# First late pair: the rectifications on ScalarE, and the next pair's inputs asked for within the fifth product

## The chip, the cores and the metric

One core of a Trainium2 chip runs the whole kernel. The metric is the device time of one execution in microseconds. The kernel before takes 769.24 us, the median of three runs (768.65 to 773.24).

## What is computed

Linear attention with a decay per head, then a block that mixes with a Fourier transform, normalises each row and applies a two-layer perceptron. All inputs are float32: q, k and v of 4 x 8 x 768 x 64, and weights of 512 x 2048 and 2048 x 512. Cut to what matters here:

```
x = attention(q, k, v, lam)                  # (4, 768, 512)
u = x + real(fft2(x))                        # over positions and channels
un = (u - mean(u)) / sqrt(var(u) + 1e-6)
out = u + maximum(un @ w_ch1, 0) @ w_ch2
```

The change lies in the last line, in the rectification `maximum(..., 0)` and in the loads of the transposed un.

## The kernel before

**The work.** The 4 x 768 rows are 24 tiles of 128 rows, taken as 12 groups of two tiles. The first four groups ("plain") go through the perceptron by direct products, interleaved with attention and Fourier mixing. The other eight ("late") make four pairs of groups, handled at the end of the kernel by `late()`. They multiply by a scheme of seven products in place of eight (Strassen's, in Winograd's form): matrices are cut into quarters, sums of quarters are formed beforehand, and the seven products are added up in a few PSUM banks.

**The first late pair** (number 0) uses one level of that scheme in its first layer, `first_layer`, lines 1223 to 1289. It loops over HF = 8 column blocks i of the hidden layer. `prod` (L1230) issues a product of 256 columns: two matmuls in the program, four matmul instructions in the trace. For each block there are three PSUM banks, X, Y and Z, and seven products:

- `begin(i)`: a11 b11 into X, which ScalarE copies out (L1251); a12 b21 into Y, which VectorE adds to that copy (L1253) and rectifies in place (L1254). The result is the quarter a11 of the hidden layer.
- the body of the loop: s2 t2 on top of X, copied out by ScalarE (L1268); s3 t3 into Z; s1 t1 on top of X, copied out by ScalarE (L1271); VectorE adds Z to that copy (L1272) and rectifies it (L1273): the quarter a22.
- `finish(i)`, one block later: s4 b22 on top of X, read with a rectification by ScalarE into a tile sv (L1240): the quarter a21; a22 t4 on top of Z, which VectorE adds to the copy of L1268 (L1242) and rectifies (L1243): the quarter a12. Then come two sums on VectorE that the second layer needs, a21 + a22 (L1244) and a11 - a21 (L1245).

Since X and Z are written on top of what they hold, TensorE may go on in such a bank only when its last reader, on ScalarE or VectorE, is through. Three blocks are begun ahead. Beside this, `keep_sums` has POOL form the sums of the second layer's weights (L1054, L1058), one set of four instructions in each of seven blocks, and SP sends them to DRAM.

**The second layer** of a pair is seven products, `deep_second(j, k)` with k from 0 to 6, each of seven small matmul groups (`seven`, L1397; a group is eight matmul instructions in the trace). After each group the function `read` takes the result out of PSUM: by a ScalarE copy (L1403) where it is the first of its target, otherwise by a VectorE add (L1405). `in_step` starts a new product every seven steps and lets the last three groups of one alternate with the first groups of the next.

**The second pair's inputs.** From product 2 of the first pair on, `read` also advances `sums_of_first`: sums of first-layer weights, eight VectorE instructions (L320) in the tile `ur`, of which six are written to DRAM by POOL's queue (L322). A sum is issued after the first, third and fifth of every seven reads. `load_u(j + 1)` then asks for the second pair's inputs, 1 MB in two requests on SP's queue (L1093), into a new tile of the same name and the same place as `ur`; it must therefore wait until those writes are done. In the kernel before it stands at the end of product 4 (k == 4), after `run(P.sums)` has used up what was left of the sums. The first VectorE instruction on these inputs is L1140, in `inputs`. SP's queue also carries the loads of three tiles `tx` for every product (`load_three`, L1104) and three writes of sums into w (`place_sums_w`, L1070).

**What sets the order.** Semaphores and the order of each engine's queue come from the Tile framework, whose planner picks by its own estimate of when each instruction becomes ready, with the written order as the priority. In the trace the order is therefore not always the written one: L1242 is written ahead of L1244 and L1245 and runs behind them. Only what is passed to `keep` (`tc.keep_in_program_order`) is pinned. Among the pinned are L1140, the loads of `place_sums_w`, and POOL's work in `keep_sums`.

Of the kernel before, what the change touches and what calls it, by code (L numbers as in the profile page):

```python
# [16 lines left out]
AF = mybir.ActivationFunctionType  # L17
ALU = mybir.AluOpType
# [59 lines left out]
def kernel(  # L78
# [10 lines left out]
    nc = tc.nc  # L89
# [51 lines left out]
    def keep(i):  # L141

        if id(i) not in pinned:
            pinned[id(i)] = i
            tc.keep_in_program_order(i)
        return i
# [4 lines left out]
    def new(pool, shape, tag, **kw):  # L151
        cnt[0] += 1
        return pool.tile(shape, F32, tag=tag, name=f"{tag}{cnt[0]}", **kw)
# [854 lines left out]
    V = nc.vector  # L1008
# [75 lines left out]
    def load_u(j, queue=nc.sync):  # L1084

        r = s2.u[j] = new(s2.up, [128, 2, KO, G * 128], "ur")
        two = LATE[2 * j:2 * j + 2]
        for h, (b, g) in enumerate(two):
            if j == PAIRS - 1:
                for i in range(G):  # L1090
                    queue.dma_start(r[:, h, :, 128 * i:128 * i + 128], utd[two[i]][:, :, 128 * h:128 * h + 128])
                continue
            i = queue.dma_start(r[:, h], utd[b, g])  # L1093
            if j == 0:
                keep(i)

    def bank():
        return new(s2.ps, [128, DM], "p2")
# [81 lines left out]
    def load_x(j):  # L1180
        P = pairs[j]
        P.us = [new(s2.yp, [128, G, DM], "u2", bufs=2) for _ in range(2)]
        for k in range(2):
            for s in range(G):
                keep(nc.sync.dma_start(P.us[k][:, s], ud[P.who[k][s]]))
# [6 lines left out]
    def split(t):  # L1192

        A11, _, A21, _ = quarters_a(t)
        keep(V.tensor_tensor(A21, A11, A21, op=SUB))
# [27 lines left out]
    def first_layer(j):  # L1223

        P = pairs[j]
        h, U = P.h, P.U

        def prod(ps, a, b, i, first):
            for kt in range(2):
                nc.tensor.matmul(ps, lhsT=s2.A[a][:, kt, 128 * i:128 * i + 128], rhs=U[b][:, kt, :],  # L1230
                                 start=(first and kt == 0), stop=(kt == 1), skip_group_check=True)

        def two(t):
            return t.rearrange("p (s k) -> p s k", s=G)

        def finish(i, X, Z):
            a11, a12, a22, s1, s3 = (h[n][:, :, i, :] for n in ("a11", "a12", "a22", "s1", "s3"))
            prod(X, "s4", "b22", i, False)
            a21 = new(s2.hp, [128, G, 128], "sv", bufs=3)
            nc.scalar.activation(a21, two(X), AF.Relu)  # L1240
            prod(Z, "a22", "t4", i, False)
            V.tensor_tensor(a12, two(Z), a12, op=ADD)  # L1242
            V.tensor_scalar(a12, a12, 0.0, None, op0=ALU.max)  # L1243
            V.tensor_tensor(s1, a21, a22, op=ADD)  # L1244
            V.tensor_tensor(s3, a11, a21, op=SUB)  # L1245

        def begin(i):
            a11 = h["a11"][:, :, i, :]
            X, Y = (bank()[:, 0:G * 128] for _ in range(2))
            prod(X, "a11", "b11", i, True)  # L1250
            nc.scalar.copy(a11, two(X))  # L1251
            prod(Y, "a12", "b21", i, True)
            V.tensor_tensor(a11, two(Y), a11, op=ADD)  # L1253
            V.tensor_scalar(a11, a11, 0.0, None, op0=ALU.max)  # L1254
            return X

        last = None
        AHEAD = 3
        begun = [begin(i) for i in range(AHEAD)]
        for i in range(HF):  # L1260
            a12, a22 = (h[n][:, :, i, :] for n in ("a12", "a22"))
            if i >= AHEAD:
                begun.append(begin(i))
            X, Z = begun[i], bank()[:, 0:G * 128]
            if last:
                finish(*last)
            prod(X, "s2", "t2", i, False)
            nc.scalar.copy(a12, two(X))  # L1268
            prod(Z, "s3", "t3", i, True)
            prod(X, "s1", "t1", i, False)  # L1270
            nc.scalar.copy(a22, two(X))  # L1271
            V.tensor_tensor(a22, two(Z), a22, op=ADD)  # L1272
            V.tensor_scalar(a22, a22, 0.0, None, op0=ALU.max)  # L1273
            last = (i, X, Z)
            if i < len(PRODUCTS):
                if i == 0:
                    keep(nc.gpsimd.tensor_copy(s2.begun, h["a11"][:, 0, 0, 0:1]))
                keep_sums(i)
            if i == HF - 3:
                load_x(j)  # L1280
            if i == HF - 2:
                for k in range(2):
                    run(prepare_b(j, k))
            if i > HF // 2:
                split(h[("a11", "a12", "s3")[i - HF // 2 - 1]])
        run(prepare_a(j, 0))
        finish(*last)
        run(prepare_a(j, 1))
        open_y(j)
# [91 lines left out]
    def deep_second(j, k):  # L1381

        P = pairs[j]
        h, (a, b) = P.h, PRODUCTS[k]
        y11, y12, y21, y22 = P.y
        if k == 0:
            P.t = new(s2.yp, [128, G, HM], "t2")
        T = P.t
        y, fresh = ((T, 1), (y11, 1), (y22, 1), (T, 0), (y12, 1), (y21, 0), (y12, 0))[k]
        A11, A12, A3, A22 = [[t[:, i] for i in range(HF // 2)] for t in quarters_a(h[a])]  # L1390
        B11, T3, B21, B22 = quarters_b(s2.B[b])
        (S1, S2, S4), (T1, T2, T4) = P.pre_a.pop(k), P.pre_b.pop(k)
        ab = [(A11, B11), (A12, B21), (S2, T2), (A3, T3), (S1, T1), (A22, T4), (S4, B22)]

        def mm(m, ps, start):
            for i in range(HF // 2):
                nc.tensor.matmul(ps[:, 0:HM // 2], lhsT=ab[m][0][i], rhs=ab[m][1][:, i, :], start=(start and i == 0),  # L1397
                                 stop=(i == HF // 2 - 1), skip_group_check=True)

        def read(ps, s, m, first):  # L1400
            o = y[:, s, m * HM // 2:(m + 1) * HM // 2]
            if first and fresh:
                nc.scalar.copy(o, ps[:, 0:HM // 2])  # L1403
            else:
                V.tensor_tensor(o, ps[:, 0:HM // 2], o, op=ADD)  # L1405
            P.reads = P.reads + 1
            if P.sums and P.reads % 7 in (1, 3, 5):
                next(P.sums, None)

        if k == 0:  # L1410
            P.reads, P.sums = 0, None
        if j < DEEP and k == 2:
            P.sums = sums_of_first()
        yield from seven(mm, read, (0, 2, 3, 5, 4, 1, 6) if (j, k) == (PAIRS - 1, 6) else range(7))

        def add_u(o, y, k, m):
            u = P.us[k][:, :, 0:HM] if m == 0 else P.us[k][:, :, DM - 1:HM - 1:-1]
            nc.gpsimd.tensor_tensor(o, y, u, op=ADD)  # L1418

        who, yt = P.who, P.yt  # L1420
        if k == 0:
            h["s2"] = h["a11"]
            if j < DEEP:
                split(h["s1"])
            part_sum(V, h["a11"], h["s1"], h["a11"], SUB)
        elif k == 1:
            V.tensor_tensor(y11, y11, T, op=ADD)  # L1427
            add_u(y11, y11, 0, 0)
        elif k == 2:
            if j < DEEP:  # L1430
                split(h["a22"])
            h["s4"] = h["a12"]
            part_sum(V, h["a12"], h["a12"], h["s2"], SUB)
            if j == DEEP - 1:
                place_sums_w()
        elif k == 3:
            V.tensor_tensor(y22, y22, T, op=ADD)
            add_u(y21, y22, 1, 0)
            add_u(T, T, 0, 1)
            add_u(y22, y22, 1, 1)  # L1440
        elif k == 4:
            V.tensor_tensor(y22, y22, y12, op=ADD)
            V.tensor_tensor(y12, y12, T, op=ADD)
            if j < DEEP:
                run(P.sums)
                load_u(j + 1)
        elif k == 5:
            store(*who[1][1], yt[:, 1, 1])
            if j == PAIRS - 1:
                store(*who[1][0], yt[:, 1, 0])  # L1450
                for s in range(G):
                    store(*who[0][s], yt[:, 0, s], slice(0, HM))
        else:
            store(*who[0][1], yt[:, 0, 1], slice(HM if j == PAIRS - 1 else 0, DM))
            if j == PAIRS - 1:
                for m in (0, HM // 2):
                    store(*who[0][0], yt[:, 0, 0], slice(HM + m, HM + m + HM // 2))
            else:
                store(*who[1][0], yt[:, 1, 0])
                store(*who[0][0], yt[:, 0, 0])  # L1460
# [88 lines left out]
    def run(gen):  # L1549
        return sum(gen)  # L1550
# [116 lines left out]
```

## Time and profile before

| | |
|---|---|
| median of three runs | 769.24 us (768.65 to 773.24) |
| the profiled execution's own time | 765.44 us |
| its span on the core | 763.7 us |
| mean granted TensorE clock | 0.999 |
| TensorE busy | 740.6 us, 97% |
| VectorE busy | 606.2 us, 79% |
| ScalarE busy | 209.2 us, 27% |
| POOL busy | 202.5 us, 27% |
| HBM | 160 GB/s over the span |

The span is one execution as the hardware profiler saw it, and the time of 765.44 us holds it and 1.7 us around it. PE is TensorE's matmul, PEld its weight load, DVE is VectorE, ACT ScalarE, SP the queue that issues most transfers. Tiles are named without numbers: ha and hs are quarters of the hidden layer, p is a PSUM bank, y and t are the second layer's results, tx, td and sd are sums of weights in SBUF and in DRAM, ur is the pair's input, utd its source in DRAM. The first layer of the first late pair runs from 401.2 to about 451 us of the span, its second layer to about 495 us. In a timeline row the columns are start, length, engine, line, operation, written and read tiles with their shapes and count, and in brackets the idle time before it with what ended it.

### The profile page before, as it was taken

To read this page: it belongs to the slowest core of one execution; us is meant where nothing else is said; L and a number is where in the kernel's file an instruction comes from. 1 tells how busy PE (TensorE), PEld (TensorE's weight loads), DVE (VectorE), ACT (ScalarE), POOL (GpSimd) and SP (SyncE) were. 2 spreads that over 40 slices of the span, in tenths; PEclk is the share of its full clock that TensorE was granted. 3 is DMA by queue.
4 is the path that set the end of the run, shared out by engine and by line. 5 is a ranking of instruction groups with operands and counts; after the bars stand their busy time and mean duration, and the time that the engine had idled before them with its cause. 6 is when DMAs were issued, how large, how long until landed. Compare 5 with 4: busy or idle time off the path is not lost.

```text
span 763.7 us, 17114 instructions
## 1 busy us (share of the span) xinstructions
PE 740.6 (97%) x6890; PEld 643.9 (84%) x6890; DVE 606.2 (79%) x1162; ACT 209.2 (27%) x487; POOL 202.5 (27%) x221
## 2 busy tenths in 40 slices
PE   7889999999999999999999999999999999999997
PEld 6788888884576586769648899999999999999997
DVE  5668967659999787587937999779986699748984
ACT  3354554553142111012002221034301341034310
POOL 3444433210042223300007922350024001320013
PEclk9999999999999999999999999999999999999999
DMA  9879986536353537522522476675645456456452
GB/s 202 247 179 228 241 247 187 176 103 190 97 168 130 127 115 207 142 93 56 124 56 97 152 221 215 220 247 180 189 125 181 142 163 190 131 170 187 140 139 69
DMA packets 132741, 123.50 MB, mean 162 GB/s; under 512 B 67007, under 2 KB 93247, under 8 KB 132663
## 3 DMA queue, kind: packets, MB, share of 16 engines
q1 hardware_dynamic: 126902, 103.66, 48.0%
q0 software_dynamic: 4032, 12.99, 5.0%
q10 hardware_dynamic: 1728, 5.77, 2.4%
q8 instruction: 54, 0.88, 0.5%
q14 instruction: 25, 0.20, 0.1%
HBM read 90.66 MB, written 31.73 MB: 160 GB/s over the span
## 4 chain that ended last, share of the span: by engine, by line
PE 47%; DVE 3%; DMA 2%; issue 1%; POOL 0%; SPq 0%; ACT 0%; DVEq 0%; POOLq 0%
PE p L1397 21%; PE p L1323 17%; PE p L1230 6%; PE pm L960 4%; DMA sd<-ur 1%; DMA ur<-utd 1%; DVE w1s L1036 1%; DMA tx<-td 0%; DVE un L792 0%; DVE e L807 0%; POOL rs L771 0%; DVE stt L766 0%; DVE hs L1245 0%; DVE hr L952 0%; DVE ha L1273 0%
## 5 line engine op out<-in xcount | busy, mean ns | idle before, releaser
L960 PE MATMUL pm<-w,hr 128*128 128x512 f32 x240 | 105.8, 594 | 0.1
L945 PE MATMUL pm<-ut,w 128*128 128x256 f32 x448 | 101.2, 380 | 1.1 <-ACT ut L871 0.7
L945 PEld LDWEIGHTS pm<-ut,w 128*128 128x128 f32 x448 | 84.0, 190 | 15.3 <-issue 3.3
L960 PEld LDWEIGHTS pm<-w,hr 128*128 128x128 f32 x240 | 44.9, 190 | 54.4 <-issue 50.9
L1418 POOL TENSOR_TENSOR y<-y,u 128x512 f32<-128x512 f32 x12 | 19.9, 1661 | 186.8 <-DVE y L1427 100.4
L1397 PE MATMUL p<-tx,sx 128*128 128x128 f32 x400 | 52.7, 275 | 0.0
L1397 PEld LDWEIGHTS p<-tx,sx 128*128 128x128 f32 x400 | 48.6, 192 | 0.0
L1332 DVE TENSOR_TENSOR ha<-p,ha 128x512 f32<-128x512 f32 x60 | 40.1, 685 | 8.3 <-PE p L1323 8.1
L1403 ACT COPY y<-p 128x128 f32<-128x128 f32 x48 | 12.8, 266 | 103.6 <-PE p L1397 103.1
L1405 DVE TENSOR_TENSOR y<-p,y 128x128 f32<-128x128 f32 x92 | 25.5, 284 | 16.1 <-PE p L1397 9.4
L954 ACT ACTIVATE hr<-pm 128x256 f32<-128x256 f32 x40 | 15.4, 385 | 81.9 <-PE pm L945 79.9
L1397 PE MATMUL p<-w,ha 128*128 128x128 f32 x288 | 37.4, 275 | 0.0
L1332 DVE TENSOR_TENSOR hs<-p,hs 128x512 f32<-128x512 f32 x39 | 26.2, 685 | 12.3 <-PE p L1323 12.3
L1397 PEld LDWEIGHTS p<-w,ha 128*128 128x128 f32 x288 | 34.9, 192 | 0.1
L267 ACT ACTIVATE e<-e,cvt 128x512 uint16<-128x512 uint16 x32 | 22.9, 721 | 40.4 <-DVE e L266 36.5
L1323 PE MATMUL p<-sx,tx 128*128 128x128 f32 x264 | 33.9, 275 | 0.0
L1323 PEld LDWEIGHTS p<-sx,tx 128*128 128x128 f32 x264 | 31.7, 192 | 0.0
L934 POOL DMA_INDIRECT out_dram<-y,ix x12 | 15.0, 1251 | 62.7 <-DVE y L997 50.7
L623 POOL DMA_INDIRECT fo<-xa,ix x6 | 15.4, 2566 | 59.1 <-DVE w L271 53.8
L1323 PE MATMUL p<-ur,w 128*128 128x128 f32 x216 | 28.0, 275 | 0.0
L435 PE MATMUL pa<-w 64*64 64x128 f32 x768 | 25.5, 271 | 2.3 <-issue 2.0
L1330 ACT COPY ha<-p 128x512 f32<-128x512 f32 x24 | 14.0, 584 | 49.2 <-PE p L1323 49.2
(342 smaller groups left out, 1932.2 us busy)
## 6 DMA issues: line engine op xcount, KB each, us to landing
tx<-td SPq DMA_DIRECT2D x84, 256.0 KB
tx<-sd SPq DMA_DIRECT2D x63, 256.0 KB
words<-in_moe_w_ch_dram SPq DMA_DIRECT2D x23, 512.0 KB
w<-in_v_dram SPq DMA_DIRECT2D x12, 512.0 KB
words<-in_k_dram SPq DMA_DIRECT2D x11, 512.0 KB
td<-tx SPq DMA_DIRECT2D x21, 256.0 KB
raw<-in_moe_w_ch_dram ACTq DMA_DIRECT2D x9, 512.0 KB
ud<-x SPq DMA_DIRECT2D x16, 256.0 KB
```

Of the source, the lines that this page charges most:

```text
L267: P(nc.scalar.activation(pw, pw, AF.Relu, bias=cvt[:, 0:1], scale=8.0))
L435: lead(P(mm(pss[r][hi][HD[ch], hp, :], lhsT=kT[HD[hi], r, hp, D * ch:D * ch + D], rhs=qT[HD[hi], hp, C * ch:C * ch + C], start=True, stop= ...
L623: P(gather(out=eo[b][a][1][0:n, 1, 0:DM], out_offset=None, in_=xa[:, :], in_offset=row_of(a, n)))
L945: P(nc.tensor.matmul(ps, lhsT=w1[:, c, 128 * fc:128 * fc + 128], rhs=ut[:, c, :], start=(c == 0), stop=(c == KO - 1)))
L954: P(nc.scalar.activation(t, ps, AF.Relu))
L960: return P(nc.tensor.matmul(ps, lhsT=hr[(fc - f0) // 4][:, fc % 4, 128 * i:128 * i + 128], rhs=w2[:, fc, :], start=(fc == f0), stop=(fc == ...
L1230: nc.tensor.matmul(ps, lhsT=s2.A[a][:, kt, 128 * i:128 * i + 128], rhs=U[b][:, kt, :], start=(first and kt == 0), stop=(kt == 1), skip_gro ...
L1323: nc.tensor.matmul(ps[:, 128 * i:128 * i + 128], lhsT=ab[m][0][:, 128 * i:128 * i + 128], rhs=ab[m][1], start=(start and i == 0), stop=Tru ...
L1332: V.tensor_tensor(o, p, o, op=ADD)
L1397: nc.tensor.matmul(ps[:, 0:HM // 2], lhsT=ab[m][0][i], rhs=ab[m][1][:, i, :], start=(start and i == 0), stop=(i == HF // 2 - 1), skip_grou ...
L1405: V.tensor_tensor(o, ps[:, 0:HM // 2], o, op=ADD)
L1418: nc.gpsimd.tensor_tensor(o, y, u, op=ADD)
```

## The change

Two things. First, the three in-place rectifications of `first_layer`, each issued eight times, are issued as a ScalarE activation (Relu) in place of a VectorE `tensor_scalar` with max. Second, `load_u(j + 1)` leaves the end of product 4: `read` now calls it at the first of its turns at which `sums_of_first` has nothing left. By the written order that is the last read of product 3, which alternates with product 4's; the end of product 4 keeps only an assertion.

```
--- before
+++ after
@@ first_layer, finish @@
             prod(Z, "a22", "t4", i, False)
             V.tensor_tensor(a12, two(Z), a12, op=ADD)
-            V.tensor_scalar(a12, a12, 0.0, None, op0=ALU.max)
+            nc.scalar.activation(a12, a12, AF.Relu)
             V.tensor_tensor(s1, a21, a22, op=ADD)
             V.tensor_tensor(s3, a11, a21, op=SUB)
@@ first_layer, begin @@
             V.tensor_tensor(a11, two(Y), a11, op=ADD)
-            V.tensor_scalar(a11, a11, 0.0, None, op0=ALU.max)
+            nc.scalar.activation(a11, a11, AF.Relu)
             return X
@@ first_layer, the loop @@
             V.tensor_tensor(a22, two(Z), a22, op=ADD)
-            V.tensor_scalar(a22, a22, 0.0, None, op0=ALU.max)
+            nc.scalar.activation(a22, a22, AF.Relu)
             last = (i, X, Z)
@@ deep_second, read @@
             P.reads = P.reads + 1
-            if P.sums and P.reads % 7 in (1, 3, 5):
-                next(P.sums, None)
+            if P.sums and P.reads % 7 in (1, 3, 5) and next(P.sums, P) is P:
+                P.sums = None
+                load_u(j + 1)
@@ deep_second @@
             V.tensor_tensor(y12, y12, T, op=ADD)
             if j < DEEP:
-                run(P.sums)
-                load_u(j + 1)
+                assert P.sums is None
         elif k == 5:
```

More of the change, by code (lines that the diff above doesn't have):

```diff
@@ L1242, in finish @@
             V.tensor_tensor(a12, two(Z), a12, op=ADD)
-            V.tensor_scalar(a12, a12, 0.0, None, op0=ALU.max)
+            nc.scalar.activation(a12, a12, AF.Relu)
             V.tensor_tensor(s1, a21, a22, op=ADD)
@@ L1253, in begin @@
             V.tensor_tensor(a11, two(Y), a11, op=ADD)
-            V.tensor_scalar(a11, a11, 0.0, None, op0=ALU.max)
+            nc.scalar.activation(a11, a11, AF.Relu)
             return X
@@ L1272, in first_layer @@
             V.tensor_tensor(a22, two(Z), a22, op=ADD)
-            V.tensor_scalar(a22, a22, 0.0, None, op0=ALU.max)
+            nc.scalar.activation(a22, a22, AF.Relu)
             last = (i, X, Z)
@@ L1406, in read @@
             P.reads = P.reads + 1
-            if P.sums and P.reads % 7 in (1, 3, 5):
-                next(P.sums, None)
+            if P.sums and P.reads % 7 in (1, 3, 5) and next(P.sums, P) is P:
+                P.sums = None
+                load_u(j + 1)
         if k == 0:
@@ L1444, in deep_second @@
             if j < DEEP:
-                run(P.sums)
-                load_u(j + 1)
+                assert P.sums is None
         elif k == 5:
```

## The prediction

> **What bounds the kernel now.** I read the page first, then the two stretches that the diff touches in the windows view, then the timeline and the chain of waits inside them.
>
> ```profile
> PE 740.6 (97%) x6890; PEld 643.9 (84%) x6890; DVE 606.2 (79%) x1162; ACT 209.2 (27%) x487; POOL 202.5 (27%) x221
> ...
> 401.20:451.50 50.30, 49.68 (x233) 43.26 (x232) 45.91 (x73) 12.01 (x32) 39.09 (x30) 1.00 0.48 167
> 451.50:475.00 23.50, 23.50 (x213) 23.50 (x212) 22.70 (x44) 3.46 (x13) 3.74 (x5) 1.00 0.52 163
> 475.00:492.00 17.00, 15.65 (x140) 15.46 (x140) 11.23 (x25) 0.80 (x3) 5.25 (x5) 1.00 0.75 252
> ```
>
> TensorE is busy for 97% of the span. The columns of the windows rows are the stretch, then PE, PEld, DVE, ACT, POOL. The first row is the first pair's first layer: VectorE works 45.91 of its 50.30 us, ScalarE only 12.01, yet PE is idle for just 50.30 - 49.68 = 0.62. The third row holds the second layer's end and the arrival of the second pair: PE is idle for 17.00 - 15.65 = 1.35. Those two idle times are nearly all that these stages can give back. A saving on VectorE counts only where it ends one of them. The clock column is 1.00 in all three.
>
> The two stalls, in the order of time:
>
> ```profile
> 412.65 1.49 DVE L1245 TENSOR_TENSOR hs<-ha,sv 128x256 f32<-128x256 f32 x1
> 413.49 0.37 ACT L1271 COPY ha<-p 128x256 f32<-128x256 f32 x1 [2.21 <-PE p L1230]
> 413.94 0.84 PEld L1230 LDWEIGHTS p<-ur,w1s 128*128 128x128 f32 x4
> 414.06 0.41 DVE L1242 TENSOR_TENSOR ha<-p,ha 128x256 f32<-128x256 f32 x1
> 414.50 0.91 DVE L1243 TENSOR_SCALAR ha<-ha 128x256 f32<-128x256 f32 x1
> 415.33 0.41 DVE L1272 TENSOR_TENSOR ha<-p,ha 128x256 f32<-128x256 f32 x1
> 415.80 0.73 PEld L1230 LDWEIGHTS p<-sx,w 128*128 128x128 f32 x4 [1.02 <-DVE ha L1272]
> ...
> 421.17 0.73 PEld L1230 LDWEIGHTS p<-sx,w 128*128 128x128 f32 x4 [0.33 <-DVE ha L1272]
> ```
>
> TensorE may not write on into the third bank (Z) until VectorE has read it in L1272. That read stands behind a rectification of 0.91 us (L1243), so the weights come 1.02 us late, and one round later 0.33 us late. After that the first layer runs without a gap.
>
> ```profile
> 472.45 5.55 SPq L1104 DMA_DIRECT2D tx<-td  x4
> 476.79 0.29 DVE L1405 TENSOR_TENSOR t<-p,t 128x128 f32<-128x128 f32 x1 [0.19 <-PE p L1397]
> 477.00 0.68 DVE L320 TENSOR_TENSOR ur<-w1s,ur 128x512 f32<-128x512 f32 x1
> 477.98 6.31 DMA sd<-ur
> 484.44 0.32 SPq L1093 DMA_DIRECT2D ur<-utd  x1
> 484.85 0.38 SPq L1104 DMA_DIRECT2D tx<-td  x1
> 485.29 0.42 SPq L1093 DMA_DIRECT2D ur<-utd  x1
> 485.29 5.15 DMA ur<-utd
> 490.56 0.69 DVE L1140 TENSOR_TENSOR ur<-ur 128x512 f32<-128x512 f32 x1 [3.49 <-DMA ur<-utd]
> 491.17 0.28 DVE L1405 TENSOR_TENSOR y<-p,y 128x128 f32<-128x128 f32 x1
> 491.51 0.97 PEld L1397 LDWEIGHTS p<-w2s,sx 128*128 128x128 f32 x8 [1.54 <-DVE y L1405]
> ```
>
> The second stall is a chain. The tile ur first holds the weight sums. Their last write to DRAM takes 6.31 us; only then may the next pair's inputs be asked for, at 484.44 and 485.29; they land 5.15 us after the second request; VectorE waits 3.49 us at L1140, in front of a bank read (L1405) that TensorE needs, and TensorE is 1.54 us late.
>
> **Part one: 24 rectifications change engine.** Removed from VectorE, from the grouped lines of the first layer:
>
> ```profile
> L1273 DVE TENSOR_SCALAR ha<-ha 128x256 f32<-128x256 f32 x8 | 6.4, 802 | 0.3
> L1243 DVE TENSOR_SCALAR ha<-ha 128x256 f32<-128x256 f32 x7 | 5.7, 821 | 0.2
> L1254 DVE TENSOR_SCALAR ha<-ha 128x256 f32<-128x256 f32 x8 | 4.7, 599 | 0.2
> 452.29 0.29 DVE L1243 TENSOR_SCALAR ha<-ha 128x256 f32<-128x256 f32 x1
> ```
>
> That is 6.4 + 5.7 + 4.7 = 16.8 us in the stage and 0.29 just behind it. The 0.29 us is what one takes when POOL is idle; most cost 0.9 because they wait for a POOL instruction to finish.
>
> Added to ScalarE: 24 instructions of a form that the trace has only at 512 elements. The copies from PSUM give the step from 512 to 256:
>
> ```profile
> L1337 ACT ACTIVATE ha<-ha x24: 629/631/635, 522.5 to 713.6; 128x512 f32<-128x512 f32 x24
> L1330 ACT COPY ha<-p 128x512 f32<-128x512 f32 x24 | 14.0, 584 | 49.2 <-PE p L1323 49.2
> L1271 ACT COPY ha<-p 128x256 f32<-128x256 f32 x8 | 3.0, 372 | 13.4 <-PE p L1230 13.4
> ```
>
> So I estimate 631 - (584 - 372) = 419 ns each (bounds 0.37 and 0.63), 24 x 0.42 = 10.1 us. ScalarE goes from 12.0 to about 22 us of 50.3, so its sum is covered; VectorE falls to 29. On TensorE's path, VectorE reaches L1272 as soon as L1242 is over, at 414.06 + 0.41 = 414.47 instead of 415.33. The weights can then follow at about 414.95 and not at 415.80, which saves 0.85; the 0.33 that follows goes too: **-1.2 us**. The bounds are no gain (another wait replaces it) and 1.02 + 0.33 = 1.35.
>
> In a sentence that the sum does not need: the Trainium skill, page "ScalarE: Activation LUTs", section "Rules for kernel authors", says that relu and max belong on VectorE and not on ScalarE. The trace agrees for an undisturbed pair (0.29 against an estimated 0.42 us) and not beside POOL (0.8 on average); by that rule the change costs 24 x 0.13 = 3.1 us of engine time, if nothing covered it.
>
> The wait that the change adds is on ScalarE: each rectification now waits for the VectorE add before it, and ScalarE's queue is served in order, so the PSUM copies behind it wait too. Here is one settled round:
>
> ```profile
> 427.57 0.38 ACT L1240 ACTIVATE sv<-p 128x256 f32<-128x256 f32 x1 [1.40 <-PE p L1230]
> 428.84 0.41 DVE L1244 TENSOR_TENSOR hs<-sv,ha 128x256 f32<-128x256 f32 x1
> 428.85 1.53 POOL L1058 TENSOR_TENSOR tx<-w2s 128x512 f32<-128x512 f32 x1
> 429.18 1.48 DVE L1245 TENSOR_TENSOR hs<-ha,sv 128x256 f32<-128x256 f32 x1
> 429.25 0.37 ACT L1268 COPY ha<-p 128x256 f32<-128x256 f32 x1 [1.29 <-PE p L1230]
> 429.91 1.03 PE L1230 MATMUL p<-sx,w1s 128*128 128x256 f32 x4
> 430.58 0.41 DVE L1242 TENSOR_TENSOR ha<-p,ha 128x256 f32<-128x256 f32 x1
> 430.97 0.37 ACT L1271 COPY ha<-p 128x256 f32<-128x256 f32 x1 [1.35 <-PE p L1230]
> ```
>
> The copy L1268 ends at 429.62, and TensorE writes the same bank again at 429.91: a margin of 0.29 us. The copy L1271 ends at 431.34, and its bank is written next after eight more matmul instructions of about 0.215 us (four take 0.84 to load), so it has over 1 us. The new rectification of a12 is ready when L1242 ends, at 430.99. If the planner puts it behind L1268, it costs at most about 0.45 us at L1271, inside the margin. That is the order I take, because in the order of this trace L1242 already comes after the copy. If the planner puts it ahead of L1268, the rivals below give the price. VectorE's two sums stay late: L1245 takes 1.48 us since it outlasts the POOL instruction that began at 428.85.
>
> Beside that row: the Trainium skill, page "SBUF — State Buffer", section "Who interferes with whom", says that a VectorE instruction with two SBUF inputs is fully blocked by a GpSimd instruction that reads SBUF and began earlier, while ScalarE never waits on anyone. The trace fits this (429.18 + 1.48 = 430.66, just past 428.85 + 1.53 = 430.38). By that rule L1245 does not get shorter when the rectifications leave.
>
> **Part two: the request moves from the fifth product's end to an earlier read.** In the written order the two requests move past seven matmul groups (at most; one group is 8 instructions in 0.89 us) and ahead of the three loads of tx for product six. But the place in the text is not what holds the request. The SP queue stood ready from 478.0 (472.45 + 5.55), and both requests waited for the sum's write, which ends at 477.98 + 6.31 = 484.29. That write cannot start sooner: its last VectorE sum (477.00) follows a read that itself waited for TensorE (0.19 at 476.79), so emptying VectorE does not move it. What remains is that the second request no longer stands behind one tx load: 485.29 - 484.85 = 0.44 us earlier, and 256 KB less ahead of it in the DMA engines, at the stage's 252 GB/s another 1 us at most. I take **-0.7 us**, between 0 and the whole stall of 1.54; a loss is possible as well, if the tx loads pushed behind 1 MB of inputs come late, bounded by the same 5.15 us of landing less the groups that TensorE still has in hand: up to about 2 us.
>
> Sum against the profiled execution: 765.44 - 1.2 - 0.7 = 763.5. Its time is 3.8 below the median of the runs shown, 769.24, so for a median the forecast is 769.24 - 1.9 = **767.3 us**.
>
> **Rivals.**
> (a) Nothing moves: the request is still gated by the write, and ScalarE's new waits take the place of the two VectorE waits. For it: 484.29 gates it whatever the text says. Against it: 1.02 of the stall is plainly L1243. 769.2 us.
> (b) A short ScalarE jam: the planner puts L1242 ahead of L1245 and the rectification ahead of L1268. L1242 then ends near 429.25 + 0.41 = 429.66, the rectification at 430.1, the copy at 430.5, that is 0.9 late less 0.29 of margin = 0.6 us a round, 8 rounds: +4.8 - 1.9, 772.1 us. For it: the rectification is written ahead of that copy.
> (c) **Slower**: the same place in ScalarE's queue, but L1242 stays behind L1245. The rectification ends at 430.99 + 0.42, the copy at 431.78, and the matmul of 429.91 starts 1.9 us late in every round: 5 to 8 rounds are 9.5 to 15 us, about 12 with the 0.7 of part two against it: 781 us. It decides from the point where the jam holds more than four rounds. For it: VectorE's present order and the 1.48 of L1245. Against it: a planner that sees L1242 that late would let the ready copy go first.
> (d) VectorE's price rules, as the page on ScalarE has it: 3.1 us uncovered, less the 0.7: 771.6 us. Against it: 38 us of ScalarE idle in the stage.
> (e) Faster by over 1%: the planner's whole order of the later pairs would have to change. PE's idle here sums to 2 us, so nothing in these rows offers 7.7.
>
> **Chances.** Forecast 0.45, (a) 0.17, (b) 0.20, (c) 0.12, (d) 0.03, (e) 0.03. One per cent (7.7 us) is about what a measurement of this kernel can tell from no change. Within it: 0.45 + 0.17 + 0.20 + 0.03 = 0.85; slower 0.12; faster 0.03. The range leaves out (c) and (e): from 764.0 (both stalls gone whole, 2.9, and the 0.6 by which the lowest run lies under the median, with some reserve) to 776.0 ((b) at 0.9 a round and the upper runs shown, up to 773.24).
>
> **What would show it.** Part one is right if no PE or PEld row in the first layer names L1272 as its releaser, VectorE is at 27 to 33 us of that stage and ScalarE at 20 to 24, with the moved instructions at 0.38 to 0.45 us. Part two is right if the two requests still start right after the last sd<-ur write and stand side by side, and the wait at L1140 shrinks from 3.49 to between 2 and 3. The prediction is wrong if ScalarE copies in the first layer wait for VectorE ahead of a PE gap (b, c), if the write's end moves with the request, or if PE shows gaps at the tx loads of product six.

## The result: 0.56% slower, and the profile after

The changed kernel takes 772.99 us (median of 20 runs, 771.31 to 777.86), the kernel before 768.65 (median of 20, 766.22 to 773.24). The ratio is 1.0056, with a 95% interval of 1.0044 to 1.0069: about 4.3 us slower, where 1.9 us faster was forecast. It lies inside 1% and inside the range, on the other side of the kernel before.

The stretches of the prediction, shifted to where they lie in the profile after, which has a span of 770.0 us (windows view; the columns are the stretch, then PE, PEld, DVE, ACT, POOL):

```profile
403.75:459.40 55.65, 50.45 (x233) 42.91 (x232) 29.61 (x51) 19.53 (x55) 37.79 (x30) 1.00 0.43 152
459.40:483.00 23.60, 23.60 (x214) 23.60 (x213) 22.46 (x43) 3.88 (x14) 3.74 (x5) 1.00 0.53 161
483.00:500.00 17.00, 17.00 (x155) 17.00 (x153) 14.00 (x32) 0.80 (x3) 6.92 (x7) 1.00 0.83 266
```

VectorE's work in the first layer fell from 45.9 to 29.6 us and ScalarE's rose from 12.0 to 19.5, as planned. Yet TensorE is idle there for 55.65 - 50.45 = 5.2 us, where it was 0.62. In the last stretch the idle time of 1.35 is gone. So one part of the change lost about 5 us and the other gained about 1.4.

What TensorE waited for in the first layer, in the timeline of its weight loads:

```profile
417.19 0.73 PEld L1230 LDWEIGHTS p<-ur,w1s 128*128 128x128 f32 x4 [0.73 <-ACT ha L1271]
422.47 0.73 PEld L1230 LDWEIGHTS p<-ur,w1s 128*128 128x128 f32 x4 [0.23 <-ACT ha L1271]
427.75 0.73 PEld L1230 LDWEIGHTS p<-sx,w1s 128*128 128x128 f32 x4 [1.96 <-ACT ha L1268]
435.71 0.73 PEld L1230 LDWEIGHTS p<-sx,w1s 128*128 128x128 f32 x4 [2.05 <-ACT ha L1268]
443.68 0.73 PEld L1230 LDWEIGHTS p<-sx,w1s 128*128 128x128 f32 x4 [2.06 <-ACT ha L1268]
449.77 0.73 PEld L1230 LDWEIGHTS p<-sx,w1s 128*128 128x128 f32 x4 [0.18 <-ACT ha L1268]
```

No row names L1272 any more. The two waits of 1.02 and 0.33 us have become two of 0.73 and 0.23 in the opening (the rounds of blocks 1 and 2), then three of about 2 us each for the copy L1268 in the settled rounds (blocks 3 to 7), and then almost nothing. In the opening the rectification L1243 stands behind the copy L1268 and in front of L1271, which waits with it:

```profile
416.47 0.42 ACT L1243 ACTIVATE ha<-ha 128x256 f32<-128x256 f32 x1 [2.63 <-DVE ha L1242]
416.79 0.35 ACT L1271 COPY ha<-p 128x256 f32<-128x256 f32 x1
```

One of the three long rounds, on all engines; here L1243 stands in front of L1268:

```profile
431.57 0.38 ACT L1240 ACTIVATE sv<-p 128x256 f32<-128x256 f32 x1
431.67 2.67 POOL L1058 TENSOR_TENSOR tx<-w2s,tx 128x512 f32<-128x512 f32 x2
431.99 1.22 DVE L1244 TENSOR_TENSOR hs<-sv,ha 128x256 f32<-128x256 f32 x1 [0.84 <-ACT sv L1240]
433.04 1.03 PE L1230 MATMUL p<-ur,w 128*128 128x256 f32 x4
433.14 1.48 DVE L1245 TENSOR_TENSOR hs<-ha,sv 128x256 f32<-128x256 f32 x1
434.54 0.41 DVE L1242 TENSOR_TENSOR ha<-p,ha 128x256 f32<-128x256 f32 x1
434.99 0.42 ACT L1243 ACTIVATE ha<-ha 128x256 f32<-128x256 f32 x1 [3.03 <-DVE ha L1242]
435.31 0.35 ACT L1268 COPY ha<-p 128x256 f32<-128x256 f32 x1
435.72 1.13 PE L1230 MATMUL p<-sx,w1s 128*128 128x256 f32 x4 [1.65 <-ACT ha L1268]
```

ScalarE stands idle for 3.03 us in front of the rectification L1243. The copy that TensorE needs is queued behind it. The rectification waits for the add L1242, and that stands in VectorE's queue behind two sums that take 1.22 and 1.48 us beside POOL. The first of the next two rows is POOL's last pair of sums, one round on; it ends at 442.38 + 2.55 = 444.93. The second is VectorE's sum in the round after that: it takes 0.42 us, and TensorE's wait is 0.18.

```profile
442.38 2.55 POOL L1058 TENSOR_TENSOR tx<-w,tx 128x512 f32<-128x512 f32 x2
...
448.26 0.42 DVE L1245 TENSOR_TENSOR hs<-ha,sv 128x256 f32<-128x256 f32 x1
```

The second pair's arrival, from SP, POOL and VectorE:

```profile
485.86 0.54 POOL L322 DMA_DIRECT2D sd<-ur  x1 [2.14 <-DMA tx<-td]
490.69 0.79 SPq L1093 DMA_DIRECT2D ur<-utd  x2
495.66 0.69 DVE L1140 TENSOR_TENSOR ur<-ur 128x512 f32<-128x512 f32 x1 [0.70 <-DMA ur<-utd]
```

Both requests go out together, 4.8 us after the last write was issued, and VectorE waits 0.70 us instead of 3.49. TensorE does not feel it.

Device times of this kernel vary by several us from one run to the next: in the twelve profiles of this study the first layer begins anywhere from 401.2 to 407.7 us, though the instructions ahead of it were not changed. So each experiment is read by two lengths inside its profile besides its time. "First layer" is from the first to the last start of a matmul instruction of L1230; "second" is from there to the first start of a matmul of L1323, the second pair's first layer.

| kernel | first layer, us | second, us | ratio to before (95%) |
|---|---|---|---|
| before | 49.94 | 42.26 | |
| before, second profile (e8) | 49.93 | 41.83 | one run |
| changed | 55.27 | 40.64 | 1.0056 (1.0044 to 1.0069) |
| e1, part two alone | 49.96 | 40.64 | 1.0004 (0.9983 to 1.0025) |
| e2, part one alone | 55.26 | 41.18 | 1.0080 (1.0049 to 1.0111) |
| e3, a12 back on VectorE | 49.31 | 40.64 | 0.9991 (0.9963 to 1.0020) |
| e4, the add first | 49.24 | 40.64 | 1.0003 (0.9979 to 1.0026) |
| e5, a12 alone on ScalarE | 56.43 | 40.64 | 1.0070 (1.0047 to 1.0094) |
| e6, the copy first | 49.56 | 40.64 | 0.9992 (0.9965 to 1.0019) |
| e7, POOL reads nothing | 49.02 | 40.64 | one run |
| e9, requests side by side | 49.95 | 40.64 | 0.9984 (0.9967 to 1.0001) |
| e10, add first, all on VectorE | 49.50 | 40.64 | 0.9982 (0.9962 to 1.0002) |

### The profile page after: what moved, and what is told of

Read it like the earlier page. It is cut to its first block, busy times and chain, and to the rows that moved or that the text cites. A ratio compares the mean times of both kernels' runs of the same rounds, so it can differ in the third digit from the quotient of the medians.

```text
span 770.0 us, 17113 instructions
## 1 busy us (share of the span) xinstructions
PE 740.8 (96%) x6890; PEld 642.6 (83%) x6890; DVE 589.7 (77%) x1138; ACT 217.1 (28%) x511; POOL 199.4 (26%) x221
## 4 chain that ended last, share of the span: by engine, by line
PE 48%; DVE 4%; ACT 1%; issue 1%; POOL 0%; DVEq 0%; POOLq 0%
PE p L1397 23%; PE p L1323 17%; PE p L1230 5%; PE pm L960 4%; DVE hs L1245 1%; DVE w1s L1036 1%; DVE hs L1244 0%; DVE un L792 0%; DVE e L807 0%; POOL rs L771 0%; DVE stt L766 0%; ACT ha L1243 0%; ACT sv L1240 0%; DVE ha L1242 0%; DVE hr L952 0%
## 5 line engine op out<-in xcount | busy, mean ns | idle before, releaser
L1405 DVE TENSOR_TENSOR y<-p,y 128x128 f32<-128x128 f32 x92 | 25.5, 284 | 16.3 <-PE p L1397 9.6
L1323 PE MATMUL p<-sx,tx 128*128 128x128 f32 x264 | 33.9, 275 | 0.0
L1323 PEld LDWEIGHTS p<-sx,tx 128*128 128x128 f32 x264 | 31.6, 192 | 0.0
L1323 PE MATMUL p<-ur,w 128*128 128x128 f32 x216 | 28.0, 275 | 0.0
```

The lines of the kernel that those rows point to most:

```text
L1323: nc.tensor.matmul(ps[:, 128 * i:128 * i + 128], lhsT=ab[m][0][:, 128 * i:128 * i + 128], rhs=ab[m][1], start=(start and i == 0), stop=Tru ...
```

## The experiments

The theory after the result: the loss is one rectification, that of a12, in front of one copy in ScalarE's queue, waiting for an add that is late because of POOL; the gain is the request. The rivals: the loss goes with the number or the length of the moved instructions; the two parts act on each other; or the request costs something.

**The two parts alone, e1 and e2.** e1 is the changed kernel with the three lines of the first layer back on VectorE; e2 has those three on ScalarE and the request in its old place.

> Part two alone: the second pair's inputs asked for early, all 24 rectifications on VectorE as before. Theory (the request is worth the stall, the loss sits in the first layer): 1.0 to 1.6 us faster than the kernel before, no TensorE wait left at L1405 near the arrival of the second pair, the first layer 50.3 us as before. Rival (the request itself costs, by holding up the loads of product six): same or up to 2 us slower, with TensorE gaps in product six.

> Part one alone: 24 rectifications on ScalarE, the request where it was before. Theory: the first layer takes 5.3 us longer as in the changed kernel and the later stall of 1.4 us stays, so 4.5 to 6 us slower than before. Rival (the two parts act on each other): less than 3 us slower.

e1: the second layer takes 40.64 us, with no TensorE wait at L1405 and none in product six. By time the gain is not to be seen (1.0004, with an interval of 0.4%); by the profile it is 1.2 to 1.6 us against the two profiles of before. e2: the first layer takes 55.3 us and the time is 1.008 of before, so the loss is part one's alone. Its later stall is smaller than expected, 0.5 us against 1.5 and 1.1 in the profiles of before. The parts add up: e2 has the first layer of the changed kernel and e1 its second. By these lengths the whole change costs 5.3 - 1.6 = 3.7 us; by the two spans it is 770.0 - 763.7 = 6.3, of which 403.75 - 401.20 = 2.55 had arisen before the first layer began.

**Which rectification, e3 and e5.** In e3 that of a12 goes back, in e5 it alone stays:

```
 e3 (against the changed kernel)
-            nc.scalar.activation(a12, a12, AF.Relu)
+            V.tensor_scalar(a12, a12, 0.0, None, op0=ALU.max)
 e5 (against the changed kernel)
-            nc.scalar.activation(a11, a11, AF.Relu)
+            V.tensor_scalar(a11, a11, 0.0, None, op0=ALU.max)
...
-            nc.scalar.activation(a22, a22, AF.Relu)
+            V.tensor_scalar(a22, a22, 0.0, None, op0=ALU.max)
```

> The changed kernel with the rectification of a12 alone (8 of 24) back on VectorE. Theory (only the rectification of a12 stands ahead of a PSUM copy that TensorE needs): the waits of TensorE for L1268 vanish, 1 to 2 us faster than before. Rival (each rectification on ScalarE costs by its longer time and its semaphores, so the loss goes with their number): two thirds of 5.3 stay, less 1.5 of the request, 2 us slower than before.

> The changed kernel with only the rectification of a12 on ScalarE; those of a11 and a22 are back on VectorE. Theory (that one rectification makes the whole jam): 3 to 6 us slower than before, the same waits of TensorE for L1268. Rival (the loss goes with the number): a third of 5.3 less 1.5, within 0.5 us of before.

With 16 of 24 rectifications still on ScalarE, e3 has no wait for a copy left and a first layer of 49.3 us. With the other 8 alone, e5 has the longest first layer of all, 56.4 us, and three waits of the same kind:

```profile
431.08 0.73 PEld L1230 LDWEIGHTS p<-sx,w1s 128*128 128x128 f32 x4 [2.21 <-ACT ha L1268]
439.05 0.73 PEld L1230 LDWEIGHTS p<-sx,w1s 128*128 128x128 f32 x4 [2.05 <-ACT ha L1268]
447.10 0.73 PEld L1230 LDWEIGHTS p<-sx,w1s 128*128 128x128 f32 x4 [2.15 <-ACT ha L1268]
```

So the loss does not go with the number of moved instructions. e5 is worse than the changed kernel probably because the rectifications back on VectorE hold L1242 up further; that was not tested by itself.

**The queue's order and the lateness, e4, e6 and e7.** e6 changes only what stands first on ScalarE, e4 only how early the add runs on VectorE, e7 only what makes the sums slow.

```
 e4, in finish
-            V.tensor_tensor(a12, two(Z), a12, op=ADD)
+            keep(V.tensor_tensor(a12, two(Z), a12, op=ADD))
             nc.scalar.activation(a12, a12, AF.Relu)
-            V.tensor_tensor(s1, a21, a22, op=ADD)
-            V.tensor_tensor(s3, a11, a21, op=SUB)
+            keep(V.tensor_tensor(s1, a21, a22, op=ADD))
+            keep(V.tensor_tensor(s3, a11, a21, op=SUB))
 e6, in the loop (a12's rectification leaves finish, but for the last block)
-            nc.scalar.copy(a12, two(X))
+            keep(nc.scalar.copy(a12, two(X)))
+            if last:
+                z = h["a12"][:, :, i - 1, :]
+                keep(nc.scalar.activation(z, z, AF.Relu))
 e7, in keep_sums
-        pin(nc.gpsimd.tensor_tensor(B12, B22, B12, op=SUB))
+        pin(nc.gpsimd.memset(B12, 0.0))
...
-            pin(nc.gpsimd.tensor_tensor(o, x, y, op=op))
+            pin(nc.gpsimd.memset(o, 0.0))
```

> The changed kernel with the VectorE add that reads Z into a12 (L1242) pinned ahead of the two sums (L1244, L1245); all rectifications on ScalarE, whose order in the settled rounds stays: sv, a12's rectification, L1268. Theory (the queue is only as bad as the add it waits for is late, and the add is late by the sums that POOL holds up): the rectification is ready in time, TensorE's waits for L1268 fall under 0.3 us each, 1.5 to 3 us faster than before. Rival (the place in ScalarE's queue alone, or the number of rectifications): 3 to 5 us slower, as the changed kernel.

> The changed kernel with a12's rectification written and pinned behind the next block's copy of a12, so that ScalarE does the copy first; VectorE's order unchanged, its add still late. Theory (the place in the queue decides): no wait of over 0.3 us for the copy of a12 in the settled rounds, at most 1 us of waits in the opening two blocks, 0 to 2 us faster than before. Rival (a late a12 costs by itself, wherever it stands): 3 us or more slower.

> The changed kernel with POOL's 28 sums of second-layer weights replaced by fills that read nothing, so the second layer's products are of zeros there and the output is not the reference's. ScalarE's and VectorE's orders are unchanged. Theory (VectorE's sums with two SBUF inputs are late because they wait for POOL instructions that read SBUF): L1245 takes 0.42 instead of 1.48 us throughout, and TensorE's waits for L1268 fall under 0.3 us. Rival (the planner's order jams by itself): the three waits of 1.7 to 2.1 us stay.

e4: ScalarE's settled order is still sv, rectification, copy, and TensorE waits for no copy; one round of it:

```profile
434.16 0.43 DVE L1242 TENSOR_TENSOR ha<-p,ha 128x256 f32<-128x256 f32 x1 [1.23 <-PE p L1230]
434.50 1.43 DVE L1244 TENSOR_TENSOR hs<-sv,ha 128x256 f32<-128x256 f32 x1
434.62 0.42 ACT L1243 ACTIVATE ha<-ha 128x256 f32<-128x256 f32 x1 [0.88 <-DVE ha L1242]
435.02 0.37 ACT L1268 COPY ha<-p 128x256 f32<-128x256 f32 x1
435.69 1.03 PE L1230 MATMUL p<-sx,w1s 128*128 128x256 f32 x4
```

The sums still take 1.4 us each, now behind the add, where nobody on TensorE's path waits for them. TensorE loses 0.51 us in all (at L1272). The 1.5 to 3 us that were expected by time do not show: the ratio is 1.0003, and its interval excludes the rival's loss of 3 to 5 us but leaves room for a gain of at most 1.6 us, where the lengths give about 2. Why the time falls short of the lengths here stays open.

e6: the add is as late as in the changed kernel, and TensorE does not mind. The rectification has the line number 1272 in this kernel, the copies 1269 and 1275:

```profile
426.54 1.48 DVE L1246 TENSOR_TENSOR hs<-ha,sv 128x256 f32<-128x256 f32 x1
426.74 0.37 ACT L1269 COPY ha<-p 128x256 f32<-128x256 f32 x1 [0.60 <-PE p L1230]
427.40 1.03 PE L1230 MATMUL p<-sx,w1s 128*128 128x256 f32 x4
427.94 0.41 DVE L1242 TENSOR_TENSOR ha<-p,ha 128x256 f32<-128x256 f32 x1
428.39 0.42 ACT L1272 ACTIVATE ha<-ha 128x256 f32<-128x256 f32 x1 [1.27 <-DVE ha L1242]
428.71 0.35 ACT L1275 COPY ha<-p 128x256 f32<-128x256 f32 x1
```

This is the order that the prediction had assumed. The next copy is a little later by it and in these rounds there is time for that. The opening keeps its waits of 0.74 and 0.23 us: there, too, the rectification stands between the two copies, it waits 2.37 and 2.73 us for its add, and the copy behind it is late for TensorE.

e7: with POOL's instructions reading nothing, every sum takes 0.42 us and the long waits are gone although ScalarE's and VectorE's orders are those of the changed kernel (grouped lines of the first layer):

```profile
L1058 POOL MEMSET tx<- 128x512 f32 x21 | 10.2, 515 | 0.1
L1244 DVE TENSOR_TENSOR hs<-sv,ha 128x256 f32<-128x256 f32 x8 | 3.4, 425 | 6.6 <-ACT sv L1240 6.6
L1245 DVE TENSOR_TENSOR hs<-ha,sv 128x256 f32<-128x256 f32 x8 | 3.3, 417 | 0.0
```

TensorE's waits for L1268 sum to 0.6 us in three. The fills are also shorter than the sums, and the last one ends at 422.3 us, before the settled rounds; so there e7 leaves VectorE without POOL beside it, and does not take away its reads alone. In the opening four of VectorE's sums do overlap fills, and are as short:

```profile
418.85 1.45 POOL L1058 MEMSET tx<- 128x512 f32 x3
419.27 0.43 DVE L1244 TENSOR_TENSOR hs<-sv,ha 128x256 f32<-128x256 f32 x1 [1.31 <-ACT sv L1240]
419.61 0.42 DVE L1245 TENSOR_TENSOR hs<-ha,sv 128x256 f32<-128x256 f32 x1
```

So three things must meet in the long waits: the rectification ahead of the copy, the add behind VectorE's sums, and POOL's sums beside them. Taking away any one of them ends those waits.

**What the request gained by, e8 and e9.** e8 is the kernel before once more. e9 is the kernel before with the request still at the end of product 4, but with a priority for the planner; in its queues only one pair of SP's transfers changes places.

```
 e9 (against the kernel before)
                 run(P.sums)
-                load_u(j + 1)
+                with tc.high_priority(200):
+                    load_u(j + 1)
```

> The kernel before, unchanged, for a second profile: how much its write of the last weight sums and the stall behind it vary. If they are a property of the program: 6.3 us for the write within 0.5, 3.5 us of wait at L1140, 1.5 us of TensorE's. If they vary from run to run: a write of 4.5 to 5 us, as in the changed kernel, and a stall under 1 us.

> The kernel before with a planner priority on load_u, still written at the end of product 4. In the queues a single thing changes: SP's second input request stands ahead of a tx load instead of behind it. Theory (the moved request gains by its neighbour in SP's queue alone, and the write gates it whatever the place in the text): the first request still goes out when the last sd<-ur write ends, 4.6 to 6.3 us after it was issued, VectorE's instruction at L1140 starts 4.8 to 5.2 us after the first request instead of 6.1 to 6.9, and no TensorE wait of over 0.3 us is left: the second layer takes 40.7 us instead of 41.9 to 42.3. Rival (the earlier place in the text counts): 6.1 us and more, a stall of 0.5 to 1.5 us as before. By time within 2 us of before either way.

In e8 the write holds SP for 5.0 us instead of 6.3, TensorE's stall is 1.1 us instead of 1.54, and VectorE waits 3.06 instead of 3.49. This lies between the two expectations: the write does vary, the stall stays. First e8, then e9, each from the first request on:

```profile
488.27 0.32 SPq L1093 DMA_DIRECT2D ur<-utd  x1
488.68 0.38 SPq L1104 DMA_DIRECT2D tx<-td  x1
489.11 0.42 SPq L1093 DMA_DIRECT2D ur<-utd  x1
495.21 0.69 DVE L1140 TENSOR_TENSOR ur<-ur 128x512 f32<-128x512 f32 x1 [3.06 <-DMA ur<-utd]
```

```profile
483.94 0.80 SPq L1093 DMA_DIRECT2D ur<-utd  x2
484.83 0.85 SPq L1104 DMA_DIRECT2D tx<-td  x2
488.72 0.69 DVE L1140 TENSOR_TENSOR ur<-ur 128x512 f32<-128x512 f32 x1 [0.87 <-DMA ur<-utd]
```

From the first request to L1140 it is 6.94 us in e8 and 4.78 in e9. Over all profiles it is 6.1 to 6.9 in the three with the load between the requests (before, e2, e8) and 4.8 to 5.2 in all nine with the requests side by side, and only the first three have a stall of TensorE (0.5 to 1.5 us). SP's wait for the write, 4.5 to 5.4 us in the nine and 5.0 to 6.3 in the three, overlaps and may add a little; but e1, whose write took 5.4 us, has no stall, and e8 and e2 have one behind 5.0 and 5.2. In e9 the second layer takes 40.64 us, as with the moved text. In its trace every engine's order is that of e1: the place in the text matters only by the order in SP's queue that it leads to, and e1's 1.0004 and e9's 0.9984 are two measurements of one order, which shows how far a time can move by itself.

**Without ScalarE, e10.** Part two, all rectifications on VectorE, and the add and the two sums pinned as in e4.

> Part two with all rectifications on VectorE and the add L1242 (and a12's rectification) ahead of the two sums. Theory (the stall of 1.3 us in the first layer comes of L1242 and L1243 standing behind sums that POOL holds up, not of which engine rectifies): at most 0.5 us of TensorE waits in the first layer, which takes 49.2 to 49.5 us as with the add first and ScalarE. Rival (VectorE is full and needs ScalarE's help): waits of 1 us or more and 49.9 us or longer.

One wait of 0.8 us is left at L1272, where 0.5 was expected at most; the first layer takes 49.5 us, the upper end of what the theory allowed. So putting the add ahead gains 0.44 us without any move to ScalarE; e4, with the move, gains 0.70. The best kernels (e3, e4, e6, e9, e10) beat the changed kernel clearly and cannot be told from the kernel before by time: the largest gain by their lengths is 0.70 in the first layer and 1.2 to 1.6 in the second, about 2 us or 0.25%, and the intervals are as wide.

## Why the prediction was wrong, step by step

- **The frame held.** Two stalls, 0.62 and 1.35 us of TensorE's idle time, were nearly all that these stages could give back (the best lengths won 0.70 and 1.62), and relieving VectorE of 16 us was worth nothing beyond them.
- **The cost of the moved instructions held:** 0.417 us each against the estimated 0.42; VectorE at 29.6 us of the stage, where 27 to 33 was given. ScalarE's 19.5 lies just under the 20 to 24 given: an instruction right behind another starts about 0.1 us before that one's end (L1268 at 435.31, while L1243 ends at 434.99 + 0.42 = 435.41), so its busy time grew by 7.5 us and not by 10.1. The price of VectorE beside POOL, "0.8 on average", is 16.8 / 23 = 0.73 over the rows shown; nothing hangs on that.
- **The step that failed** is the place of a12's rectification in ScalarE's queue: "If the planner puts it behind L1268, it costs at most about 0.45 us at L1271, inside the margin. That is the order I take". The planner put it ahead of L1268 in every settled round (blocks 3 to 7). The reason given for the choice, that L1242 runs after the copy in the trace, took the measured time for the planner's. L1242 is late in the trace because of POOL, and the planner's order does not follow that lateness; it gave TensorE, VectorE and ScalarE the very same order in e7, where POOL holds nobody up, so its estimate seems to leave POOL's hold out (seen from outside, not from its workings). Where the prediction's order was forced (e6), the outcome that it gave came out in the settled rounds: no wait there.
- **Rival (c) was the mechanism**, down to its price: 1.9 us a round was worked out, and 1.96, 2.05 and 2.06 were measured. Its number of rounds was wrong. It counted 5 to 8, but POOL's sums end after the third settled round, so only three rounds paid in full. With 0.96 in the opening and 0.18 later the waits sum to 7.2 us, against 1.35 before; a group of four weights that comes late loads in 0.73 us instead of 0.84, which gives back some of it, and the first layer grew by 5.3. Rival (b) named a time close to the measured one by another mechanism, which did not occur in the jammed rounds.
- **The first stall** (-1.2) did go from L1272, but in the opening 0.96 us of waits for L1271 came in its place; its lower bound, "another wait replaces it", had named such a case. This happened in the very order that it had assumed, with the rectification behind L1268. Its "over 1 us" of margin at L1271 is that of a settled round. In the opening, in its own rows of the kernel before, that copy ends at 413.49 + 0.37 = 413.86 and TensorE loads the next weights for the bank at 413.94. The term was also too large: 1.2 is taken from waits of weight loads, while TensorE's matmuls stood idle for 0.62. In the assumed order (e6) the first layer gains 0.38 us, and at most 0.70 with all rectifications on ScalarE and POOL's sums in place (e4).
- **Part two was mis-sized:** 0.7 was taken, and 1.2 to 1.6 us came, the stall whole. That the write gates the request, and that the gain lies in the second request no longer standing behind a load, held (e9). The 0.44 us of issue was right. The landing was mis-sized: from the second request to L1140 it took 5.3 to 6.1 us with that load ahead, and about 4.6 without it. VectorE's wait at L1140 fell to 0.70, where 2 to 3 was given; of these 2.8 us about 1.2 is the shorter way from the first request to L1140 (4.97 us instead of 6.12), and 1.6 is the write, which held SP for 4.7 us instead of 6.3 and varies from run to run: that part is luck.
- **The page of the Trainium skill on ScalarE** ("ScalarE: Activation LUTs", "Rules for kernel authors"), by which these instructions belong on VectorE, did not decide it, and neither did rival (d): e3 leaves 16 of them on ScalarE at no loss, and the loss came from the place of the other 8 in the queue. **The Trainium skill's page "SBUF — State Buffer"**, "Who interferes with whom", by which VectorE's sums with two SBUF inputs are held up by a POOL instruction that reads SBUF and not by one that only writes it, agrees with these traces: 0.42 us in the four sums of e7 beside fills, 1.22 and 1.48 beside POOL sums.

## What to carry to other kernels

Before an instruction is moved to an engine that has time to spare, look at what its queue will hold up: an instruction that waits for another engine blocks every PSUM copy behind it, and an engine that was idle for 38 of 50 us became the cause of a 5 us loss. If the order is a planner's, pin it, or pin what makes the waiting instruction ready; the measured lateness of a producer need not be what the planner believes. And when a request waits in a queue, its neighbours there matter more than where it is written.

## What the runs show of the hardware

- A 128x256 sum of two SBUF tiles on VectorE takes 0.42 us beside POOL fills (four sums, e7) and up to 1.48 beside POOL sums that read SBUF; a POOL fill of 128x512 takes 0.52 us, a sum 1.3.
- A single 256 KB load between two 512 KB requests of one queue put off VectorE's use of them at L1140 by 1.4 us on average (6.4 us after the first request, in three profiles, against 5.0 in nine), more than its 0.44 us of issue.
